# Pairing the two signs of a key feature map in one stationary operand, so that a key-value product moves 65 columns instead of 129

## The chip, the cores and the metric

The kernel runs on one core of one Trainium2 chip. The metric is device time of one execution in microseconds (us), of which several are taken for each kernel, always beside executions of the kernel before on the same chip. The profile also records the mean clock that the throttle granted to TensorE, as a share of full speed (1.000). "PE" is TensorE, "PEld" its weight load, DVE is VectorE, ACT ScalarE, POOL GpSimd, SP SyncE.

## The reference, cut to what matters

Four residual blocks on x of 2048 tokens by 512: attention, feed-forward, attention, feed-forward. The attention is linear, with 32 heads of 16 and two softmaxes of opposite sign as feature map:

```python
pk = jnp.einsum("bhsd,hdf->bhsf", k, w_phi)
phi_k = jnp.concatenate([_softmax(pk, axis=-1), _softmax(-pk, axis=-1)], axis=-1)
kv = jnp.einsum("bhsf,bhsd->bhfd", phi_k, v)        # the key-value products
z  = jnp.einsum("bhsf->bhf", phi_k)
num = jnp.einsum("bhqf,bhfd->bhqd", phi_q, kv)
den = jnp.einsum("bhqf,bhf->bhq", phi_q, z)[..., None] + 1e-6
o = num / den
```

`num` needs the finished `kv`, a sum over all 2048 tokens. Everything after it in the layer waits for the last token tile.

## The kernel before

The kernel is written as a list of operations with the resources that they read and write. A list scheduler in the kernel file orders all of them by given durations, and semaphores are made from that order. So any edit may move every operation.

For each of the 16 token tiles of an attention layer: layer norm, a transpose by DMA, key and value projections (PE), exp with both signs and a copy of v (ACT), the softmax sums and reciprocals (DVE), the multiply that normalises (POOL; for tiles 14 and 15 one half on POOL, one on DVE), then eight key-value products (PE):

```python
    def kv_acc(self, t, tag):
        for g in range(NG):                      # 8 groups: sign s, 8 heads c
            s, c = g // 4, g % 4
            bank, j = g // 3, g % 3              # PSUM banks 0, 1, 2
            op("pe", ... e.matmul(
                k.pb[bank][:, j * 130:j * 130 + 129], k.expk[:, t, s, c * 128:(c + 1) * 128], k.vsb[:, t, c, 0:129],
                start=(t == 0 and j == 0), stop=(t == NT - 1), ...),
               [r("phik", t, s), r("v", t), r("vones")], [self.RP[bank]], 59, f"{tag} kvacc {t} {g}")
```

The stationary operand holds 8 heads of 16 features, the moving one 8 heads of 16 values and a column of ones for `z`. Only the 8 diagonal blocks of the 128x128 result are wanted. The finishing step takes them out of PSUM with a mask, bank by bank:

```python
    def kv_fin(self, tag):
        for bank in range(3):
            ...
            op("dve", ... k.kvbd[:, g0:g0 + n, 0:128] ... pv[:, :, 0:128] ... k.mask8 ..., ALU.mult),
               [self.RP[bank], r("mask8")], [r("kvbd", bank)], 550 if n == 3 else 430, f"{tag} kvbd {bank}")
            op("dve", ... k.kvbd[:, g0:g0 + n, 128:136] ... pv[:, :, 128:129] ..., ALU.add, ALU.mult),
               [self.RP[bank], r("mask8"), r("kvbd", bank)], [r("kvbd", bank)], 200, f"{tag} kvden {bank}")
```

The step runs on DVE once per attention layer. It lets `num` start, and it gives banks 0, 1, 2 back to the query projections, which write to banks 0 to 3.

The softmax here doesn't subtract the row's maximum and nothing guards it: scores larger than these inputs give would overflow.

## Time and profile before

392.31 us in the median of 3 executions (391.47 to 392.65).

From the profile page of the kernel before, engines' busy time and then the chain of work that ended last, by engine:

```profile
PE 379.4 (97%) x2331; PEld 208.0 (53%) x2331; DVE 272.0 (70%) x547; ACT 206.6 (53%) x389; POOL 168.5 (43%) x284
PE 88%; POOL 4%; ACT 3%; DMA 2%; DVE 1%; issue 1%; ACTq 0%; POOLq 0%
```

The timeline at the end of the second attention layer's key phase, kernel before (start, duration, engine and line, what it writes and reads, count, and in brackets the idle time before it with what ended it; L634 is the normalising multiply, L663 the products, L674 and L679 the finishing step, L690 query projections, L706 `num`):

```profile
236.69 1.50 POOL L634 TENSOR_TENSOR expk<-expk,rZk 128x512 bf16<-128x512 bf16 x1 [0.95 <-DVE rZk L631]
237.22 2.77 PE L663 MATMUL ps<-vsb,expk 128*128 128x129 bf16 x45
238.70 1.08 DVE L674 TENSOR_TENSOR kvbd<-ps,mask 128x384 bf16<-128x384 f32 x2 [1.43 <-PE ps L663]
239.70 0.30 DVE L679 SCALAR_TENSOR_TENSOR kvbd<-ps,mask 128x24 bf16<-128x24 f32 x2
239.83 0.38 PE L690 MATMUL ps<-yT,Wqp 128*128 128x512 bf16 x1
240.03 0.42 DVE L674 TENSOR_TENSOR kvbd<-ps,mask 128x256 bf16<-128x256 f32 x1
240.04 0.54 PE L706 MATMUL ps<-kvbd,expq 128*128 128x144 bf16 x6
240.49 0.17 DVE L679 SCALAR_TENSOR_TENSOR kvbd<-ps,mask 128x16 bf16<-128x16 f32 x1
```

How to read it. A matmul's record is long (217 to 231 ns for a product), but records overlap; the cost of one in a row is start to start: 45 products from 237.22 to 239.83 us are 58 ns each. The finishing step begins at 238.70 us, 1.1 us before PE is through with the products and turns to its next matmul (239.83 us), because bank 0 was complete. PE never stops: products, one query projection, then `num`.

### The profile page before, as it was taken

How to read it: one execution, taken by the hardware profiler on the slowest of the kernel's cores; microseconds unless marked ns; L12 is line 12 of the kernel's file. 1: busy time of each engine (PE TensorE's matmuls, PEld its weight loads, DVE VectorE, ACT ScalarE, POOL GpSimd, SP SyncE). 2: the span in 40 equal slices, each digit the busy share in tenths (PEclk: the TensorE clock that was granted, in tenths of full speed). 3: DMA queues.
4: the chain of work that ended last, by engine and by line, in shares of the span. 5: the costliest groups of instructions: out<-in, count | busy, mean ns of one | idle time of the engine just before them, and what ended most of it. 6: DMA issues, size and time to landing. Idle time of an engine off the chain costs nothing.

```text
span 390.3 us, 6397 instructions
## 1 busy us (share of the span) xinstructions
PE 379.4 (97%) x2331; PEld 208.0 (53%) x2331; DVE 272.0 (70%) x547; ACT 206.6 (53%) x389; POOL 168.5 (43%) x284
## 2 busy tenths in 40 slices
PE   5999989999999999999999999999999999999997
PEld 3445554667644544444444457567774554444444
DVE  4999978877766888866766777897986776232222
ACT  5898859834633404533453484985563462553340
POOL 5499936641724363372244543584553242100000
DMA  6833682311311322401000110132323132100002
GB/s 179 228 67 71 191 299 53 69 40 32 53 40 27 43 55 44 84 10 28 14 15 0 27 29 3 40 80 57 55 55 69 27 42 67 29 14 27 17 12 67
DMA packets 61663, 23.01 MB, mean 59 GB/s; under 512 B 53472, under 2 KB 60608, under 8 KB 61632
## 3 DMA queue, kind: packets, MB, share of 16 engines
q1 hardware_dynamic: 60912, 22.02, 24.4%
q10 hardware_dynamic: 720, 0.59, 0.5%
q8 instruction: 18, 0.29, 0.3%
q14 instruction: 13, 0.11, 0.1%
HBM read 7.91 MB, written 2.10 MB: 26 GB/s over the span
## 4 chain that ended last, share of the span: by engine, by line
PE 88%; POOL 4%; ACT 3%; DMA 2%; DVE 1%; issue 1%; ACTq 0%; POOLq 0%
PE ps L758 39%; PE ps L785 19%; PE ps L617 7%; PE ps L737 7%; PE ps L690 6%; PE ps L706 4%; PE ps L663 3%; PE ps L648 2%; POOL expk L634 2%; ACT expq L693 2%; DVE stats L551 1%; DMA x_sb<-in_A_x_dram 1%; DMA hT<-in_A_wqkv_dram 1%; ACT expk L620 1%; POOL rstd L576 1%
## 5 line engine op out<-in xcount | busy, mean ns | idle before, releaser
L758 PE MATMUL ps<-yT,Wg 128*128 128x512 bf16 (+3 forms) x440 | 130.1, 337 | 0.5 <-DMA yT<-ytile 0.2
L758 PE MATMUL ps<-yT,Wu 128*128 128x512 bf16 (+3 forms) x440 | 129.6, 336 | 0.0
L760 ACT ACTIVATE gate_sb<-ps 128x512 bf16<-128x512 f32 (+3 forms) x110 | 55.9, 512 | 105.3 <-PE ps L758 102.9
L785 PE MATMUL ps<-Wd,hT 128*128 128x512 bf16 (+2 forms) x363 | 106.8, 373 | 0.0
L634 POOL TENSOR_TENSOR expk<-expk,rZk 128x1024 bf16<-128x1024 bf16 (+1 forms) x32 | 59.5, 1878 | 37.1 <-DVE rZk L631 19.7
L758 PEld LDWEIGHTS ps<-yT,Wg 128*128 128x128 bf16 (+1 forms) x440 | 43.4, 100 | 33.8 <-issue 1.1
L758 PEld LDWEIGHTS ps<-yT,Wu 128*128 128x128 bf16 (+1 forms) x440 | 43.7, 100 | 32.6 <-ACT expk L765 0.2
L767 DVE TENSOR_TENSOR hT<-gate_sb,expk 128x512 bf16<-128x512 bf16 (+3 forms) x73 | 29.8, 409 | 37.9 <-ACT expk L765 33.0
L785 PEld LDWEIGHTS ps<-Wd,hT 128*128 128x128 bf16 (+1 forms) x363 | 35.3, 98 | 36.6 <-DVE x_sb L787 0.6
L551 DVE BATCH_NORM_STATS2 stats<-x_sb 128x6 f32<-128x512 bf16 x64 | 42.6, 682 | 5.5 <-DMA x_sb<-in_A_x_dram 5.1
L366 ACT ACTIVATE numbf<-ps 128x432 bf16<-128x432 f32 x64 | 33.1, 536 | 19.5 <-PE ps L706 19.4
L629 DVE TENSOR_REDUCE Zk<-expk 128x64 f32<-128x1024 bf16 x32 | 37.7, 1194 | 5.7 <-ACT expk L620 5.4
L731 POOL TENSOR_TENSOR osb<-tsc 128x512 bf16<-128x512 bf16 x28 | 32.5, 1162 | 19.9 <-DVE tsc L726 17.8
L737 PE MATMUL ps<-wo_p,oT 128*128 128x512 bf16 x128 | 39.8, 379 | 0.0
L770 DVE TENSOR_TENSOR hT<-gate_sb,ps 128x512 bf16<-128x512 bf16 (+2 forms) x37 | 22.7, 613 | 20.8 <-PE ps L758 19.6
L693 ACT ACTIVATE expq<-ps 128x1024 bf16<-128x1024 f32 (+1 forms) x40 | 32.6, 861 | 7.3 <-PE ps L690 7.0
L765 ACT ACTIVATE expk<-ps 128x512 bf16<-128x512 f32 (+3 forms) x73 | 36.1, 497 | 0.1
L706 PE MATMUL ps<-kvbd,expq 128*128 128x144 bf16 x256 | 35.0, 226 | 0.5 <-ACT numbf L366 0.5
L620 ACT ACTIVATE expk<-ps 128x512 bf16<-128x512 f32 x44 | 23.9, 598 | 21.5 <-PE ps L617 21.2
L690 PE MATMUL ps<-yT,Wqp 128*128 128x512 bf16 x128 | 34.6, 379 | 0.6 <-ACT expq L693 0.5
L787 DVE TENSOR_TENSOR x_sb<-x_sb,ps 128x512 bf16<-128x512 bf16 (+1 forms) x33 | 22.0, 669 | 18.8 <-PE ps L785 18.4
L559 POOL TENSOR_TENSOR rstd<-rv,mhalf 128x1 f32<-128x1 f32 (+1 forms) x53 | 31.9, 607 | 2.9
(73 smaller groups left out, 429.2 us busy)
## 6 DMA issues: line engine op xcount, KB each, us to landing
out_dram<-x_sb SPq DMA_DIRECT2D x15, 128.0 KB, 1.7
x_sb<-in_A_x_dram SPq DMA_DIRECT2D x3, 512.0 KB, 6.2
Wu<-in_B_W_up_dram SPq DMA_DIRECT2D x4, 344.0 KB, 5.9
Wg<-in_B_W_gate_dram SPq DMA_DIRECT2D x4, 344.0 KB, 5.5
Wd<-in_B_W_down_dram SPq DMA_DIRECT2D x5, 256.0 KB, 6.9
yT<-ytile SPq DMA_TRANSPOSE x60, 2.5
hT<-in_A_wqkv_dram ACTq DMA_DIRECT2D x4, 128.0 KB, 3.1
x_sb<-in_A_x_dram SPq DMA_DIRECT2D x4, 128.0 KB, 3.7
```

Of the source, the lines that this page charges most:

```text
L366: return e.activation(out, in_, ACT.Copy) if hasattr(e, "activation") else e.tensor_copy(out, in_)
L551: op("dve", (lambda t: lambda e: e.bn_stats(k.stats6[:, t, :], k.x_sb[:, t, :]))(t), [r("x", t)], [r("st", t)], 685, f"{tag} stats {t}")
L629: op("dve", lambda e: e.tensor_reduce(k.Zk[:, zb, :], k.expk[:, t, :, :].rearrange("p s (h f) -> p (s h) f", f=16), AX.X, ALU.add), [r("ex ...
L634: op(eng, (lambda s0, s1: lambda e: e.tensor_tensor(k.expk[:, t, s0:s1, :].rearrange("p s (h f) -> p (s h) f", f=16), k.expk[:, t, s0:s1, ...
L690: op("pe", (lambda c, ic, bank: lambda e: e.matmul(k.pb[bank][:], k.Wqp[:, ic, c * 128:(c + 1) * 128], k.yT[:, ic, st * 512:(st + 1) * 512 ...
L693: op("act", (lambda c0, s, b0: lambda e: e.activation(k.expq[:, st, c0:c0 + w, s, :], k.ps[:, b0:b0 + w, :], ACT.Exp, scale=(1.0 - 2.0 * s ...
L706: op("pe", (lambda s, c, j, g0, bank: lambda e: e.matmul(k.pb[bank][:, j * GW:(j + 1) * GW], k.expq[:, st, c, s, tt * 128:(tt + 1) * 128], ...
L737: op("pe", (lambda c, bank: lambda e: e.matmul(k.pb[bank][:], k.oT[:, ob, c, :], k.wo_p[:, c, :], start=(c == 0), stop=(c == NC - 1)))(c, ...
L758: op("pe", (lambda bank, W, ic, fc, Mf: lambda e: e.matmul(k.pb[bank][0:Mf, 0:n], W[:, ic, fc * 128:fc * 128 + Mf], k.yT[:, ic, c0:c0 + n] ...
L760: op("act", (lambda Mf, gb, gs: lambda e: e.activation(k.gate_sb[0:Mf, gs, 0:n], k.pb[gb][0:Mf, 0:n], ACT.Relu))(Mf, gb, gs), [self.RP[gb] ...
L765: op("act", (lambda Mf, ub, tu: lambda e: e.activation(k.expk[0:Mf, tu, 0, 0:n], k.pb[ub][0:Mf, 0:n], ACT.Copy))(Mf, ub, tu), [self.RP[ub] ...
L785: op("pe", (lambda fc, Kf, u, c0, bank, m0, m1: lambda e: e.matmul(k.pb[bank][:, m0:m1], k.hT[0:Kf, u, c0:c0 + 128], k.Wd[0:Kf, fc, m0:m1] ...
```

## The change

Intent: put both signs of four heads (2 x 64 features) into one stationary operand. The moving operand then needs the values of four heads and the ones, 65 columns instead of 129. The number of products stays, their accumulators fit in two banks (0, 1), and bank 2 comes free.

The price is in the finishing step. The rows of a product are now (sign, head of 4), while `num` wants rows of 8 heads per sign, so half of the blocks move by 64 partitions: four multiplies of 64 partitions and four small ones for the denominators, and each reads both banks.

The diff, cut to its core:

```diff
-        sb("expk", [NT, 2, 512])
-        sb("vsb", [NT, NC, 130])
+        sb("expk", [NT, NG, 2, 64])
+        sb("vsb", [NT, NG, 66])
@@ kv_acc
-            s, c = g // 4, g % 4
-            bank, j = g // 3, g % 3
...
-                k.pb[bank][:, j * 130:j * 130 + 129], k.expk[:, t, s, c * 128:(c + 1) * 128], k.vsb[:, t, c, 0:129],
+            bank, col = g // 4, (g % 4 // 2) * 256 + (g % 2) * 66
...
+                k.pb[bank][:, col:col + 65], k.expk[:, t, g, :, :].rearrange("p s m -> p (s m)"), k.vsb[:, t, g, 0:65],
...
-               [r("phik", t, s), r("v", t), r("vones")], [self.RP[bank]], 59, f"{tag} kvacc {t} {g}")
+               [r("phik", t, bank), r("v", t), r("vones")], [self.RP[bank]], KVD, f"{tag} kvacc {t} {g}")    # KVD = 40.0
@@ kv_fin
-        for bank in range(3):
...
-               [self.RP[bank], r("mask8")], [r("kvbd", bank)], 550 if n == 3 else 430, f"{tag} kvbd {bank}")
+        for s in range(2):
+            for u in range(2):
+                src = k.ps[s * 64:s * 64 + 64, 0:2, :] ... u * 66:u * 66 + 65
+                dst = k.kvbd[u * 64:u * 64 + 64, s * 4:s * 4 + 4, :]
...
+                   [self.RP[0], self.RP[1], r("mask4")], [r("kvbd", s, u)], 420, f"{tag} kvbd {s} {u}")
...
+                   [self.RP[0], self.RP[1], r("mask4"), r("kvbd", s, u)], [r("kvbd", s, u)], 200, f"{tag} kvden {s} {u}")
@@ first query projection of the first layer
-        kr0, qr0 = cycle([4, 5, 6, 7]), cycle([3])
+        kr0, qr0 = cycle([4, 5, 6, 7]), cycle([2, 3])
```

Left out: the same new layout in the exps, sums, copies and multiplies, and two setup operations on POOL (a mask, zeros).

More of the change, by code (lines that the diff above doesn't have):

```diff
@@ L360 @@
 EPS_DEN = 1e-6
+KVD = 40.0
 WINDOW = {"sp": 24, "act": 64, "pe": 400, "dve": 40, "pool": 24}
@@ L427, in alloc @@
         sb("mask8t", [8])
+        sb("mask4", [4])
         sb("phi_c", [NC, DH])
@@ L496, in setup @@
         op("pool", lambda e: e.memset(k.aggw[:, 1:2], 1.0 / D), [], [r("aggw")], 100, "agg w1")
-        op("pool", lambda e: e.memset(k.vsb[:, :, :, 128:130], 1.0), [], [r("vones")], 250, "v ones")
+        op("pool", lambda e: e.memset(k.vsb[:, :, :, 64:66], 1.0), [], [r("vones")], 250, "v ones")
+        op("pool", lambda e: e.tensor_tensor(k.mask4[:], k.mask8[:, 0:4], k.mask8[:, 4:8], ALU.add), [r("mask8")], [r("mask4")], 150, "mask4")
+        op("pool", lambda e: e.memset(k.kvbd[:], 0.0), [], [r("kvones")] + [r("kvbd", s, u) for s in range(2) for u in range(2)], 1000, "kvbd zero")
         op("pool", lambda e: e.tensor_copy(k.kvbd[:, :, 136:144], k.mask8[:].unsqueeze(1).to_broadcast([P, NG, 8])), [r("mask8")], [r("kvones")], 230, "kv ones")
@@ L619, in kv_proj @@
         for s in range(2):
-            op("act", (lambda s: lambda e: e.activation(k.expk[:, t, s, :], k.pb[bk][:], ACT.Exp, scale=(1.0 - 2.0 * s)))(s),
+            op("act", (lambda s: lambda e: e.activation(k.expk[:, t, :, s, :], k.pb[bk][:].rearrange("p (g m) -> p g m", g=NG), ACT.Exp, scale=(1.0 - 2.0 * s)))(s),
                [self.RP[bk]], [r("expk", t, s)], 605, f"{tag} expk {t} {s}")
-        op("act", lambda e: e.activation(k.vsb[:, t, :, 0:128], k.pb[bv][:].rearrange("p (c n) -> p c n", c=4), ACT.Copy),
+        op("act", lambda e: e.activation(k.vsb[:, t, :, 0:64], k.pb[bv][:].rearrange("p (g n) -> p g n", g=NG), ACT.Copy),
            [self.RP[bv]], [r("v", t)], 600, f"{tag} vcopy {t}")
@@ L628, in knorm @@
         zb, rb = t % 2, t % 4
-        op("dve", lambda e: e.tensor_reduce(k.Zk[:, zb, :], k.expk[:, t, :, :].rearrange("p s (h f) -> p (s h) f", f=16), AX.X, ALU.add),
+        op("dve", lambda e: e.tensor_reduce(k.Zk[:, zb, :], k.expk[:, t, :, :, :].rearrange("p g s (h f) -> p (g s h) f", f=16), AX.X, ALU.add),
            [r("expk", t, 0), r("expk", t, 1)], [r("Zk", zb)], 1215, f"{tag} Zk {t}")
@@ L632, in knorm @@
         parts = [("pool", 0, 2)] if t < NT - 2 else [("pool", 0, 1), ("dve", 1, 2)]
-        for eng, s0, s1 in parts:
-            op(eng, (lambda s0, s1: lambda e: e.tensor_tensor(
-                k.expk[:, t, s0:s1, :].rearrange("p s (h f) -> p (s h) f", f=16),
-                k.expk[:, t, s0:s1, :].rearrange("p s (h f) -> p (s h) f", f=16),
-                k.rZk[:, rb, s0 * 32:s1 * 32].unsqueeze(2).to_broadcast([P, (s1 - s0) * 32, 16]), ALU.mult))(s0, s1),
-               [r("expk", t, s) for s in range(s0, s1)] + [r("rZk", rb)], [r("phik", t, s) for s in range(s0, s1)],
-               (1930 if s1 - s0 == 2 else 980) if eng == "pool" else 1050, f"{tag} phik {t} {s0}")
+        for eng, u0, u1 in parts:
+            n = (u1 - u0) * 32
+            kv = k.expk[:, t, u0 * 4:u1 * 4, :, :].rearrange("p g s (h f) -> p (g s h) f", f=16)
+            op(eng, (lambda kv, u0, n: lambda e: e.tensor_tensor(
+                kv, kv, k.rZk[:, rb, u0 * 32:u0 * 32 + n].unsqueeze(2).to_broadcast([P, n, 16]), ALU.mult))(kv, u0, n),
+               [r("expk", t, 0), r("expk", t, 1), r("rZk", rb)], [r("phik", t, u) for u in range(u0, u1)],
+               (1930 if n == 64 else 980) if eng == "pool" else 1050, f"{tag} phik {t} {u0}")
     def kv_pair(self, t, ring, tag):
@@ L650, in kv_pair @@
         for s in range(2):
-            op("act", (lambda s: lambda e: e.activation(k.expk[:, t:t + 2, s, :], k.ps[:, kb[0]:kb[0] + 2, :], ACT.Exp, scale=(1.0 - 2.0 * s)))(s),
+            op("act", (lambda s: lambda e: e.activation(k.expk[:, t:t + 2, :, s, :], k.ps[:, kb[0]:kb[0] + 2, :].rearrange("p b (g m) -> p b g m", g=NG), ACT.Exp, scale=(1.0 - 2.0 * s)))(s),
                [self.RP[b] for b in kb], [r("expk", tt, s) for tt in ts], 1030, f"{tag} expk {t} {s}")
-        op("act", lambda e: e.activation(k.vsb[:, t:t + 2, :, 0:128], k.ps[:, vb[0]:vb[0] + 2, :].rearrange("p b (c n) -> p b c n", c=4), ACT.Copy),
+        op("act", lambda e: e.activation(k.vsb[:, t:t + 2, :, 0:64], k.ps[:, vb[0]:vb[0] + 2, :].rearrange("p b (g n) -> p b g n", g=NG), ACT.Copy),
            [self.RP[b] for b in vb], [r("v", tt) for tt in ts], 1030, f"{tag} vcopy {t}")
@@ L660, in kv_acc @@
         for g in range(NG):
-            s, c = g // 4, g % 4
-            bank, j = g // 3, g % 3
-            op("pe", (lambda s, c, bank, j: lambda e: e.matmul(
-                k.pb[bank][:, j * 130:j * 130 + 129], k.expk[:, t, s, c * 128:(c + 1) * 128], k.vsb[:, t, c, 0:129],
-                start=(t == 0 and j == 0), stop=(t == NT - 1), skip_group_check=True))(s, c, bank, j),
-               [r("phik", t, s), r("v", t), r("vones")], [self.RP[bank]], 59, f"{tag} kvacc {t} {g}")
+            bank, col = g // 4, (g % 4 // 2) * 256 + (g % 2) * 66
@@ L668, in kv_fin @@
+            op("pe", (lambda g, bank, col: lambda e: e.matmul(
+                k.pb[bank][:, col:col + 65], k.expk[:, t, g, :, :].rearrange("p s m -> p (s m)"), k.vsb[:, t, g, 0:65],
+                start=(t == 0 and g % 4 == 0), stop=(t == NT - 1), skip_group_check=True))(g, bank, col),
+               [r("phik", t, bank), r("v", t), r("vones")], [self.RP[bank]], KVD, f"{tag} kvacc {t} {g}")
     def kv_fin(self, tag):
         op, r, k = self.op, self.r, self
-        for bank in range(3):
-            g0 = bank * 3
-            n = min(3, NG - g0)
-            pv = k.pb[bank][:, 0:n * 130].rearrange("p (g m) -> p g m", m=130)
-            op("dve", (lambda g0, n, pv: lambda e: e.tensor_tensor(
-                k.kvbd[:, g0:g0 + n, 0:128].rearrange("p g (d h) -> p g d h", h=8),
-                pv[:, :, 0:128].rearrange("p g (h d) -> p g d h", h=8),
-                k.mask8[:].unsqueeze(1).unsqueeze(1).to_broadcast([P, n, 16, 8]), ALU.mult))(g0, n, pv),
-               [self.RP[bank], r("mask8")], [r("kvbd", bank)], 550 if n == 3 else 430, f"{tag} kvbd {bank}")
-            op("dve", (lambda g0, n, pv: lambda e: e.scalar_tensor_tensor(
-                k.kvbd[:, g0:g0 + n, 128:136], pv[:, :, 128:129].to_broadcast([P, n, 8]), 0.5 * EPS_DEN,
-                k.mask8[:].unsqueeze(1).to_broadcast([P, n, 8]), ALU.add, ALU.mult))(g0, n, pv),
-               [self.RP[bank], r("mask8"), r("kvbd", bank)], [r("kvbd", bank)], 200, f"{tag} kvden {bank}")
@@ new lines, in kv_fin @@
+        for s in range(2):
+            for u in range(2):
+                src = k.ps[s * 64:s * 64 + 64, 0:2, :].rearrange("p b (c m) -> p (b c) m", c=2)[:, :, u * 66:u * 66 + 65]
+                dst = k.kvbd[u * 64:u * 64 + 64, s * 4:s * 4 + 4, :]
+                mk = k.mask4[s * 64:s * 64 + 64, :]
+                op("dve", (lambda src, dst, mk, u: lambda e: e.tensor_tensor(
+                    dst[:, :, 0:128].rearrange("p c (d h) -> p c d h", h=8)[:, :, :, u * 4:u * 4 + 4],
+                    src[:, :, 0:64].rearrange("p c (h d) -> p c d h", h=4),
+                    mk.unsqueeze(1).unsqueeze(1).to_broadcast([64, 4, 16, 4]), ALU.mult))(src, dst, mk, u),
+                   [self.RP[0], self.RP[1], r("mask4")], [r("kvbd", s, u)], 420, f"{tag} kvbd {s} {u}")
+                op("dve", (lambda src, dst, mk, u: lambda e: e.scalar_tensor_tensor(
+                    dst[:, :, 128 + u * 4:132 + u * 4], src[:, :, 64:65].to_broadcast([64, 4, 4]), 0.5 * EPS_DEN,
+                    mk.unsqueeze(1).to_broadcast([64, 4, 4]), ALU.add, ALU.mult))(src, dst, mk, u),
+                   [self.RP[0], self.RP[1], r("mask4"), r("kvbd", s, u)], [r("kvbd", s, u)], 200, f"{tag} kvden {s} {u}")
@@ L708, in num @@
                     start=(j == 0), stop=True, skip_group_check=True))(s, c, j, g0, bank),
-                   [r("expq", st, c, s), r("kvbd", gb), r("kvones")], [self.RP[bank]], 63, f"{tag} num {t} {g0 + j}")
+                   [r("expq", st, c, s), r("kvbd", s, 0), r("kvbd", s, 1), r("kvones")], [self.RP[bank]], 63, f"{tag} num {t} {g0 + j}")
             op("dve" if gb == 2 else "act", (lambda g0, n, bank: lambda e: evac(
@@ L763, in step @@
                 tu = 12 + u % 4
-                ru = [r("expk", tu, 0), r("phik", tu, 0)]
-                op("act", (lambda Mf, ub, tu: lambda e: e.activation(k.expk[0:Mf, tu, 0, 0:n], k.pb[ub][0:Mf, 0:n], ACT.Copy))(Mf, ub, tu),
+                ru = [r("expk", tu, 0), r("expk", tu, 1), r("phik", tu, 0)]
+                up = k.expk[:, tu, 0:4, :, :].rearrange("p g s m -> p (g s m)")
+                op("act", (lambda Mf, ub, up: lambda e: e.activation(up[0:Mf, 0:n], k.pb[ub][0:Mf, 0:n], ACT.Copy))(Mf, ub, up),
                    [self.RP[ub]], ru, 170 + n * 0.833, f"{tag} up {ts[0]} {fc}")
-                op("dve", (lambda Mf, tu, gs, u: lambda e: e.tensor_tensor(k.hT[0:Mf, u, 0:n], k.gate_sb[0:Mf, gs, 0:n], k.expk[0:Mf, tu, 0, 0:n], ALU.mult))(Mf, tu, gs, u),
+                op("dve", (lambda Mf, up, gs, u: lambda e: e.tensor_tensor(k.hT[0:Mf, u, 0:n], k.gate_sb[0:Mf, gs, 0:n], up[0:Mf, 0:n], ALU.mult))(Mf, up, gs, u),
                    [r("gate", gs)] + ru, [r("hT", u)], 150 + n * 0.535, f"{tag} h {ts[0]} {fc}")
```

## The prediction

> **What bounds the kernel now.** One core, granted clock 1.000, span 390.3 us. TensorE is listed busy 379.4 us (97%), and the chain that ended last is 88% PE. The key-value products (256 MATMULs of 129 moving columns, half per attention layer) are 2.8% of that chain. In the timeline, 45 of them in a row take 2.61 us (from 237.22): 58 ns each, though each record is 220 ns long. Together: 256 x 58 ns = 14.8 us of TensorE.
>
> The layers differ. In the first (20 to 53 us) POOL is full: its 1.9 us normalisation of expk runs back to back (9 in 16.21 us from 35.78), and the products wait for it; only the last 14, at 52.1 us, stand in the chain. In the second (224.7 to 239.8 us) PE has no gap: 128 products interleaved with projections, ending in the burst of 45. There each nanosecond counts, as long as the chain ACT exp -> DVE sum and reciprocal (1.22 + 0.55 us) -> POOL multiply (1.93 us) for tiles 12 to 15 keeps up.
>
> **Removed.** 64 moving columns per product, not one product: still 256 pairs of weight load and matmul. In proportion 65 columns take 58 x 65/129 = 29 ns, but each product still loads 128 stationary columns. The Trainium skill ("TensorE: Matmul & The Clock Gate", Back-to-back issue gap) says that spacing is set by both instructions, pipelined; this trace shows only that the load's limit is at most 58 ns. My estimate: 40 ns (30 to 54), so 18 ns saved per product: 2.3 us per layer.
>
> **Added.** (a) The finishing step on DVE: before, 3 multiplies (552, 552, 420 ns) and 3 small ones (174 ns), the first starting before the last product was done. After: 4 multiplies of 64 x 256 elements (estimate 420 ns, as the 128x256 one) and 4 small ones, all waiting for both banks. DVE's total is about equal; the first num matmul comes an estimated 0.5 us later, partly covered by query projections. (b) Two POOL setup operations, about 1.2 us; POOL waits for DMA at 2.2 to 3.4 us, so free.
>
> **Moved.** Bank 2 comes free: the first query projection gets two banks, and projections into banks 2 and 3 can run before the finishing step. ACT sits idle 1.5 us before its 54.08 us and 2.4 us before its 240.43 us evacuation, and is 93% busy at 250 to 260 us; an early 1.0 us exp or two fits there. Estimate 0.5 us per layer.
>
> **Sum.** Second layer: -2.3 (products) -0.5 (early exps) +0.4 (finishing) = -2.4 us. First layer: -0.3 -0.5 +0.4 = -0.4 us. The list scheduler reorders everything: +-1.5 us by chance; I add -0.5 us for shorter chains in the second layer. Total about -3.3 us: 389.0 us, 8 in 10 within 386.2 to 391.6. Faster by over 2%: 0.05; within: 0.93; slower by over 2%: 0.02.
>
> **What would show each step.** Burst of products in the timeline: near 40 ns apart (58 = load-bound, 30 = load hidden). From the first product of the second layer to its first num (224.7 to 240.0, 15.3 us) about 2.4 us shorter; the first layer's num start (53.7 us) within 0.7 us. The feed-forward stretches (95 to 215, 270 to 390 us) unchanged in length. Expq on ACT between last product and first numbf.
>
> **What would make it wrong.** Weight loads at 50 ns or more (saving under 1 us). The POOL/DVE chain of tiles 12 to 15 becoming the limit. The finishing step exposed for 1 us or more per layer. A worse order from the scheduler, or a second benefit of the freed bank that I don't see.

## More of the kernel before

How much PE waited for the multiply in the whole run, from the view of waits on PE, kernel before (total us, times, longest):

```profile
PE ps L663 <- POOL expk L634: 0.6, 1, 0.6
```

## The result, and the profile after

The changed kernel gives the right result and takes 395.95 us in the median (394.68 to 396.61, 4 executions), beside 392.27 us for the kernel before: slower by 0.9%. The ratio is 1.0089, with a 95% interval of 1.0067 to 1.011.

The four executions had clocks 0.991 (396.61 us), 0.996 (396.29 and 395.60) and 1.000 (394.68). So there are two losses: about 2.4 us at full clock, and 1 to 2 us more when the clock dropped.

The profile page of the changed kernel: busy time, the granted clock in 40 slices (tenths), the chain by engine:

```profile
PE 376.9 (95%) x2331; PEld 202.0 (51%) x2331; DVE 271.8 (69%) x551; ACT 205.7 (52%) x389; POOL 173.3 (44%) x286
PEclk9999889999999999999999999999999999999999
PE 80%; POOL 6%; DVE 6%; DMA 3%; issue 3%; ACT 1%; SPq 0%; POOLq 0%; DVEq 0%; ACTq 0%
```

PE fell from 88% to 80% of the chain, and DVE rose from 1% to 6%. First, did the products become shorter? The timeline of PE, changed kernel, first layer (L666 the products, L694 a query projection):

```profile
44.81 0.53 PE L666 MATMUL ps<-vsb,expk 128*128 128x65 bf16 x12
45.18 0.38 PE L694 MATMUL ps<-yT,Wqp 128*128 128x512 bf16 x1
```

Twelve products from 44.81 to 45.18 us: 31 ns each. That is better than predicted (40 ns): 27 ns x 256 = 6.9 us of PE are saved. And still the kernel is slower.

The same place of the second layer as shown of before, timeline of the changed kernel (L640 multiply, L626 copy of v, L678 and L683 finishing step, L710 `num`):

```profile
240.16 1.50 POOL L640 TENSOR_TENSOR expk<-expk,rZk 128x512 bf16<-128x512 bf16 x1 [0.95 <-DVE rZk L635]
241.57 0.60 ACT L626 ACTIVATE vsb<-ps 128x512 bf16<-128x512 f32 x1 [1.16 <-PE ps L666]
242.22 0.32 PEld L666 LDWEIGHTS ps<-vsb,expk 128*128 128x128 bf16 x8 [0.29 <-ACT vsb L626]
242.26 0.41 PE L666 MATMUL ps<-vsb,expk 128*128 128x65 bf16 x8
242.74 1.32 DVE L678 TENSOR_TENSOR kvbd<-ps,mask 64x256 bf16<-64x256 f32 x3 [2.00 <-PE ps L666]
244.09 0.36 DVE L683 SCALAR_TENSOR_TENSOR kvbd<-ps,mask 64x16 bf16<-64x16 f32 x2
244.48 0.43 DVE L678 TENSOR_TENSOR kvbd<-ps,mask 64x256 bf16<-64x256 f32 x1
244.51 0.42 PE L710 MATMUL ps<-kvbd,expq 128*128 128x144 bf16 x4 [1.84 <-DVE kvbd L683]
244.94 0.38 DVE L683 SCALAR_TENSOR_TENSOR kvbd<-ps,mask 64x16 bf16<-64x16 f32 x2
```

The finishing step starts only when all products are done. It takes 2.6 us (242.74 to 245.32), and PE stands still for 1.84 us of it before the first `num`. The view of waits on PE has this as its largest entry, and a second new one, a late transpose in the first layer:

```profile
PE ps L710 <- DVE kvbd L683: 3.7, 3, 1.8
PE ps L652 <- DMA yT<-ytile: 2.2, 1, 2.2
```

In this execution the stops were followed by a lower clock. Four windows of the changed kernel (columns: window, its length, busy time of PE, PEld, DVE, ACT, POOL with counts, granted clock, DMA share, GB/s):

```profile
40.00:46.00 6.00, 6.00 (x41) 2.81 (x42) 3.89 (x5) 3.91 (x5) 5.12 (x3) 0.72 0.44 105
56.00:60.00 4.00, 3.19 (x16) 1.81 (x17) 2.09 (x9) 1.90 (x5) 0.00 (x0) 0.65 0.52 162
40.20:43.40 3.20, 3.20 (x9) 1.20 (x8) 1.46 (x2) 1.60 (x2) 3.20 (x3) 0.50 0.39 104
57.30:60.40 3.10, 3.10 (x14) 1.72 (x15) 1.41 (x5) 1.00 (x3) 0.00 (x0) 0.50 0.20 62
```

Each dip follows stops of PE: the wait for the transpose (2.2 us) ended at 39.97 us, the waits for the first layer's finishing step (1.39 and 0.45 us) at 56.35 and 57.23 us. At clock 0.72 and 0.65, 6 us and 4 us hold about 1.7 us and 1.4 us less of PE. The last two lines show that the clock is 0.50 in the dips, each about 3.4 us long. The traces of r4, r5 and r16 below have one such dip each, also at a stop of PE. From this an estimate: a dip is some 1.7 us of lost clock, 0.4% of the run, so a mean clock of 0.996 is one dip, 0.991 two, 0.987 three. But a stop does not always bring a dip: r2's trace has the same wait for the transpose (2.3 us) at clock 1.000.

Where the 4.6 us between the two profiled spans (390.3 and 394.9 us) arise, read from the two timelines:

| moment, us | before | after | difference |
|---|---|---|---|
| first layer: last POOL multiply ends | 51.99 | 53.50 | +1.5 |
| finishing step ends | 54.29 | 57.17 | +2.9 |
| first feed-forward product | 72.12 | 76.39 | +4.3 |
| second layer: last POOL multiply ends | 238.19 | 241.66 | +3.5 |
| finishing step ends | 240.66 | 245.32 | +4.7 |
| first feed-forward product | 257.82 | 263.34 | +5.5 |
| span | 390.3 | 394.9 | +4.6 |

The feed-forward block between the layers gave 0.8 us back, the last one 0.9 us. From the last POOL multiply to the end of the finishing step the two layers took 2.30 and 2.47 us before, 3.67 and 3.66 us after. Not all of that growth is the step's own. In the new order the last products wait for something else: in the second layer for the copy of v, which ends at 242.17 us, 0.51 us after the multiply (shown above), and in the first for the half of a multiply that DVE does, which ends at 54.05 us, 0.55 us after POOL's:

```profile
51.17 2.88 DVE L640 TENSOR_TENSOR expk<-expk,rZk 128x512 bf16<-128x512 bf16 x2
54.10 0.43 PE L666 MATMUL ps<-vsb,expk 128*128 128x65 bf16 x8 [0.56 <-DVE expk L640]
```

Counted from these moments the step ends after 3.12 and 3.15 us, 0.8 and 0.7 us more than before.

### The profile page after: what moved, and what is told of

It reads as the page before. It is cut to its first block, busy times and chain, and to the rows that moved or that the text cites. A ratio compares the mean times of both kernels' runs of the same rounds, so it can differ in the third digit from the quotient of the medians. Undisturbed runs are those within 1.5% of the kernel's fastest.

```text
span 394.9 us, 6391 instructions
## 1 busy us (share of the span) xinstructions
PE 376.9 (95%) x2331; PEld 202.0 (51%) x2331; DVE 271.8 (69%) x551; ACT 205.7 (52%) x389; POOL 173.3 (44%) x286
## 4 chain that ended last, share of the span: by engine, by line
PE 80%; POOL 6%; DVE 6%; DMA 3%; issue 3%; ACT 1%; SPq 0%; POOLq 0%; DVEq 0%; ACTq 0%
PE ps L762 39%; PE ps L790 19%; PE ps L621 7%; PE ps L741 5%; PE ps L694 4%; PE ps L710 3%; DMA yT<-ytile 2%; PE ps L666 1%; DVE stats L555 1%; POOL rstd L563 1%; POOL osb L735 1%; PE ps L652 1%; POOL expk L640 1%; DMA x_sb<-in_A_x_dram 1%; DVE kvbd L678 1%
## 5 line engine op out<-in xcount | busy, mean ns | idle before, releaser
L790 PE MATMUL ps<-Wd,hT 128*128 128x512 bf16 (+2 forms) x363 | 103.1, 373 | 0.0
L640 POOL TENSOR_TENSOR expk<-expk,rZk 128x1024 bf16<-128x1024 bf16 (+1 forms) x32 | 59.1, 1863 | 38.0 <-DVE rZk L635 29.4
L735 POOL TENSOR_TENSOR osb<-tsc 128x512 bf16<-128x512 bf16 x28 | 33.5, 1199 | 15.5 <-DVE tsc L730 14.6
L741 PE MATMUL ps<-wo_p,oT 128*128 128x512 bf16 x128 | 38.8, 379 | 0.8 <-DMA oT<-osb 0.7
L710 PE MATMUL ps<-kvbd,expq 128*128 128x144 bf16 x256 | 33.9, 231 | 5.0 <-DVE kvbd L683 3.7
L694 PE MATMUL ps<-yT,Wqp 128*128 128x512 bf16 x128 | 36.5, 390 | 0.0
L562 POOL TENSOR_SCALAR rv<-mv 128x1 f32<-128x1 f32 (+1 forms) x53 | 13.2, 250 | 50.1 <-DVE mv L557 49.9
```

The lines of the kernel that those rows point to most:

```text
L640: op(eng, (lambda kv, u0, n: lambda e: e.tensor_tensor(kv, kv, k.rZk[:, rb, u0 * 32:u0 * 32 + n].unsqueeze(2).to_broadcast([P, n, 16]), AL ...
L694: op("pe", (lambda c, ic, bank: lambda e: e.matmul(k.pb[bank][:], k.Wqp[:, ic, c * 128:(c + 1) * 128], k.yT[:, ic, st * 512:(st + 1) * 512 ...
L710: op("pe", (lambda s, c, j, g0, bank: lambda e: e.matmul(k.pb[bank][:, j * GW:(j + 1) * GW], k.expq[:, st, c, s, tt * 128:(tt + 1) * 128], ...
L735: op(sm, lambda e: e.tensor_tensor(k.osb[:, b, :], k.tsc[:, b, 0:512], k.tsc[:, b, 512:1024], ALU.add), [r("tsc", b)], [r("osb", b)], 418 ...
L741: op("pe", (lambda c, bank: lambda e: e.matmul(k.pb[bank][:], k.oT[:, ob, c, :], k.wo_p[:, c, :], start=(c == 0), stop=(c == NC - 1)))(c, ...
L790: op("pe", (lambda fc, Kf, u, c0, bank, m0, m1: lambda e: e.matmul(k.pb[bank][:, m0:m1], k.hT[0:Kf, u, c0:c0 + 128], k.Wd[0:Kf, fc, m0:m1] ...
```

## The experiments

Theory A, structural: products of early tiles only fill PE while a chain of other engines runs for the last tiles, so shorter products shorten nothing, while the later and longer finishing step lies on the chain. Theory B, the order: the scheduler made a worse order, which shows in the late transpose and the clock. Theory C: the clock drop comes from PE idling, whatever causes that.

To hold the order fixed, many kernels replace the scheduler by a table of the operations' names:

```diff
-            prog.schedule()
+            prog.fixed(ORDER)      # order from a table; an operation that comes too early for its
+                                   # dependencies is put right after the last of them
```

All kernels, in us. "Full clock" is the mean of the executions at clock 0.999 or more.

| kernel | what | median | ratio (95%) | at full clock |
|---|---|---|---|---|
| after | the change | 395.95 | 1.0089 (1.0067 to 1.011) | 394.68 (1 of 4) |
| r1 | after, old order | 397.89 | 1.0126 (1.0096 to 1.0157) | 394.67 (2 of 6) |
| r2 | after, half the finishing | 393.83 | 1.0053 (1.004 to 1.0067) | 393.67 (4 of 6) |
| r3 | after, 129 columns | 398.28 | 1.0171 (1.0151 to 1.019) | 397.92 (3 of 5) |
| r4 | after, query ring as before | 395.58 | 1.0082 (1.0059 to 1.0104) | 393.85 (2 of 6) |
| r5 | before, 65 columns only | 391.44 | 0.9998 (0.9981 to 1.0016) | 391.48 (5 of 6) |
| r6 | r1 with useless matmuls | 395.85 | 1.0104 (1.0088 to 1.0121) | 395.79 (4 of 4) |
| r7 | after, 4 finishing operations | 395.43 | 1.0101 (1.0075 to 1.0127) | 395.03 (4 of 6) |
| r8 | before, 3 finishing operations | 392.32 | 1.0017 (1.0003 to 1.003) | 392.40 (6 of 6) |
| r9 | after, other banks | 395.30 | 1.0084 (1.0044 to 1.0124) | 394.82 (4 of 5) |
| r10 | before, other banks | 393.33 | 1.0034 (0.9993 to 1.0075) | 392.99 (5 of 6) |
| r11 | after, three mends | 391.84 | 0.9987 (0.9964 to 1.001) | 392.21 (7 of 7) |
| r12 | before, new order | 403.76 | 1.0292 (1.0257 to 1.0328) | 402.34 (2 of 6) |
| r13 | before, late finishing only | 394.50 | 1.0066 (1.005 to 1.0082) | 394.51 (6 of 6) |
| r14 | r1, 4 finishing operations | 394.11 | 1.0053 (1.0038 to 1.0068) | 393.88 (4 of 6) |
| r15 | r1, finishing by bank | 394.28 | 1.0057 (1.004 to 1.0075) | 394.25 (6 of 6) |
| r16 | r9, one look | 395.09 | none (one run) | none (clock 0.996) |
| r17 | after, three mends, four banks | 397.49 | 1.0139 (1.0118 to 1.0159) | 394.95 (1 of 5) |

### r1: the change in the old order

The edit is the table above with the order of the kernel before, the new finishing operations in the places of the old ones. (A few products of one tile trade places, since they share banks otherwise.)

> The changed kernel, but every engine issues its operations in the order that the kernel before had (the order comes from a table; the new finishing operations stand where the old ones stood). Theory A (the finishing step, which now starts only after the last product and must be done before the first num, is exposed: about 1.2 us more per layer than before): even in the old order the gain of the products is eaten, 391.5 to 394 us, and the trace shows PE idle for 1 us or more between last product and first num in both layers. Theory B (the loss is the scheduler's new order, which puts a layer-norm apply late, starves PE at 37 us and drops its clock): 389 us or less, clock 1.000, no 2 us wait for a yT transpose.

Measured: 394.50 and 394.84 us at clock 1.000, and 397.76 to 398.13 us in four executions at 0.986 to 0.991. The wait of 2.2 us for a transpose was gone (0.5 us left), and the kernel was no faster. PE stood idle before the first `num` for 0.75 us in the first layer and 1.20 us in the second (1 us or more was expected in both), and the time lies above the expected range. So the new order (theory B) is not needed for the loss. That the old order suits the new operations is not shown (see r12). At full clock the loss to the kernel before, whose median in those rounds was 391.76 us, is 2.9 us.

### r2: half of the finishing step

```diff
-            for u in range(2):
+            for u in range(1):                     # in kv_fin, after's own order
-        ... e.memset(k.kvbd[:], 0.0)
+        ... e.memset(k.kvbd[:], 1.0)               # keeps the denominators from zero
```

> The changed kernel in its own order, with only half of the finishing step (the u = 1 operations left out; wrong result on purpose). Theory A: first num about 0.9 us earlier after the last product in each layer, and the whole time 1.5 to 2.5 us less than the changed kernel's 395.95 us. Theory B: less than 0.7 us changed.

Measured: wrong result; 393.83 us in the median, 2.1 us under the change, as theory A expected. But at full clock the gain is 1.0 us (393.67 against one execution at 394.68). The rest is clock: four of six executions held full clock, against one of four (whether by the shorter step or by chance is not shown). The step is on the path, for part of its length.

### r3: 129 columns again

```diff
-                k.pb[bank][:, col:col + 65], ..., k.vsb[:, t, g, 0:65],
+                k.pb[bank][:, col:col + 129], ..., k.vsb[:, t, min(g, 6):min(g, 6) + 2, :] ... [:, 0:129],
```

> The changed kernel in its own order, with 129 moving columns per product again (wrong result on purpose; addresses and number of matmuls else the same). Products then take 58 ns instead of 31 ns, 27 ns x 256 = 6.9 us of PE. If PE were the limit while they run: the second layer 3.4 us longer, 399 us or more. If other engines' chains set when the last product can run (theory A's second half): under 1.5 us longer, 396 to 397.5 us.

Measured: 398.28 us; at full clock 3.2 us over the change. Neither expectation was met: 6.9 us more of PE cost about half of it. In this order, planned for 40 ns per product, products of 58 ns seem to hold others up; which, was not traced. That says nothing about the reverse in the kernel before, which r5 tests.

### r4: the query projection in one bank

```diff
-        kr0, qr0 = cycle([4, 5, 6, 7]), cycle([2, 3])
+        kr0, qr0 = cycle([4, 5, 6, 7]), cycle([3])
```

> The changed kernel, rescheduled, with the first query projection in bank 3 alone as before. If the second bank brings query exps between the key exps on ACT and so delays POOL (third theory): 1 us or more faster than 395.95 us. Theory A: within 1 us of it, unless the order happens to move the late layer-norm apply (theory B), which would show as no wait for yT near 37 us and clock 1.000.

Measured: 395.58 us, within 1 us of the change (393.85 us at full clock, in two executions, against one at 394.68). Its new order has no wait for a transpose near 37 us, and the kernel is still slow. The second bank for the first query projection is not the main cause.

### r5: the saving alone

```diff
-                k.pb[bank][:, j * 130:j * 130 + 129], ..., k.vsb[:, t, c, 0:129],
+                k.pb[bank][:, j * 130 + 64:j * 130 + 129], ..., k.vsb[:, t, c, 64:129],   # in the kernel before, its order
```

> The kernel before, in its own order, with its old layout and old finishing step; only the products move 65 columns instead of 129 (columns 64 to 128 of each; wrong result on purpose). This is the saving of the change alone, 256 x 27 ns = 6.9 us of PE, without its cost. Filler theory (the products of tiles 0 to 11 only fill PE while the chain LN - transpose - key projection - exp - sum - multiply of the last tiles runs, so a shorter product shortens nothing): at most 1.2 us faster than 391.76 us, and PE idle of 2 us or more appears before the last products. If PE bound the second layer as the prediction had it: 3 us or more faster, under 388.8 us.

Measured: 391.44 us beside 391.82 us, ratio 0.9998. This is 6.9 us of PE taken out of the kernel before, at no other cost, and nothing clear of the noise came of it (the interval allows -0.7 to +0.6 us). The timeline of PE shows where a part of it went (L806 products, L777 the POOL multiply), second layer, and then its view of waits:

```profile
237.06 0.74 PE L806 MATMUL ps<-vsb,expk 128*128 128x65 bf16 x19
238.93 0.95 PE L806 MATMUL ps<-vsb,expk 128*128 128x65 bf16 x26 [1.14 <-POOL expk L777]
```

```profile
PE ps L806 <- POOL expk L777: 3.2, 4, 1.1
```

The wait for the multiply, 0.6 us in the kernel before, became 3.2 us; the rest of the 6.9 us is not so easily found, since it is spread over shorter waits, some matmul records are missing (2289 of 2331), and this execution had one dip of the clock, at 52 to 55 us. PE had looked gap-free because the scheduler had put the products of earlier tiles into the time in which the last tiles' chain runs. They were filler. Only the products behind the last multiply count: here 26 of them, and 26 x 27 ns = 0.7 us.

### r6: useless matmuls where PE waits

```diff
+    def fill(self, n, tag):      # writes a bank that nobody reads
+        for i in range(n):
+            self.op("pe", lambda e: e.matmul(k.pb[2][:], k.yT[:, 0, 0:128], k.Wkp[:, 0, :], start=True, stop=True), ..., 216, f"{tag} {i}")
+        # r1, q ring [3]; 3 before the products of tiles 12 and 14 of the first layer, 5 after the last product of both
```

> r1 (changed kernel in the old order; five of its runs in two groups: 394.5 and 394.8 us at clock 1.000, 397.8 to 398.1 us at 0.986 to 0.991) with 16 useless 512-column matmuls put on PE where it waits: 3 before the products of tile 12, 3 before those of tile 14, 5 after the last product of each layer (first query projection in bank 3 only, so that bank 2 is free). Clock theory (PE idle around 47 to 55 us makes the clock gate halve the clock): clock 1.000 in all runs and 394 to 395.3 us although PE has 3.5 us more work. If idle is not the cause: two groups as in r1, each the same or up to 3 us slower.

Measured: clock 1.000 in all four executions, 395.35 to 396.11 us. r1 had kept full clock in two of six. The median is 2 us below r1's, with more work on PE, but just above what was expected (394 to 395.3 us). The first layer's critical stretch, r1 at full clock and then r6 (columns as in the windows above):

```profile
46.00:56.70 10.70, 6.90 (x84) 4.04 (x83) 7.34 (x14) 4.31 (x9) 5.27 (x4) 1.00 0.95 333
```

```profile
46.00:56.70 10.70, 9.00 (x93) 5.18 (x93) 7.34 (x14) 4.29 (x9) 5.28 (x4) 1.00 0.93 327
```

PE was busy 6.90 us of 10.70 without the filler and 9.00 us with it. That supports theory C, that PE idling itself takes the clock down, but does not show it: four executions against six are few, r6 also has the other query ring, and both of these traces are at clock 1.00. Against r1 at full clock r6 is 1.1 us slower; which of the fillers cost that was not tested.

### r7 and r8: denominators by the same multiply

```diff
-        sb("vsb", [NT, NG, 66])
+        sb("vsb", [NT, NG, 68])                    # a column of ones per head: 4 x 17 columns
-                k.pb[bank][:, col:col + 65]
+                k.pb[bank][:, col:col + 68]
-                ... four multiplies of 64x256, four of 64x16
+                ... four multiplies of 64x272, denominators among them
```

r8 does the same to the kernel before (136 columns, 3 operations instead of 6). Both are rescheduled.

> The changed kernel, rescheduled, with the denominators made by the same multiply as the numerators (v with a column of ones per head, 68 moving columns, scheduled as 31 ns): 4 finishing operations instead of 8 per layer. Exposed-finishing theory: first num 0.7 to 0.9 us after the last product instead of 1.9 us; 1.5 to 2.5 us faster than the changed kernel (393.5 to 394.5 us), still not faster than before. If the finishing step does not matter: 395 us or more.

> The kernel before, rescheduled, with the denominators made in the same way (136 moving columns): 3 finishing operations instead of 6. Here the step is mostly hidden, so 0 to 1 us faster than 391.76 us; if the finishing step were exposed here too, 1 us or more.

Measured: r7 395.43 us, a miss, with executions from 394.50 to 398.12. Its step is 0.7 us shorter, but the new order had the first layer's last POOL multiply end at 54.54 us in its profile, against 53.50 us in the changed kernel. Two things moved together, so r7 tells nothing; r14 repeats it in a fixed order. r8: 392.32 us beside 391.82, if anything slower (1.0003 to 1.003), where 0 to 1 us faster was expected. No gain of halving the operations shows where the step is mostly hidden; but r8 is rescheduled too, so this is weak.

### r9, r10, r16: a shorter chain for the last tiles

```diff
-                return [...] + [lambda t=t: self.kv_proj(t, mring, "A2") for t in tiles(st)]
+                return [...] + [lambda t=t: self.kv_proj(t, k3ring if st == 3 else mring, "A2") for t in tiles(st)]
+            k3ring = cycle([4, 5])                 # mring = cycle([6, 7]), shared with a query projection
```

r9 is the change with this edit and 31 ns per product in the scheduler; r10 is the kernel before with it; r16 is r9 again, for its trace.

> The changed kernel, rescheduled with 31 ns per product, with one more edit: in the second layer the projections of tiles 12 to 15 write to banks 4 and 5 instead of 6 and 7, which the first query projection uses too at that time. Chain theory (the time to the first num is the chain of the last four tiles' key projection, exp, sum and multiply, and only a shorter chain can turn shorter products into time): last POOL multiply to come 2 us or more earlier after the last feed-forward product than in the changed kernel, 1.5 to 3 us faster than 395.95 us in runs of equal clock. If products or the finishing step alone were the limit: within 0.7 us of the changed kernel.

> The kernel before, rescheduled, with the same edit of banks. There the products, at 58 ns, fill PE in that stretch, so a shorter chain finds no free PE: within 0.8 us of 391.8 us. If the banks alone were the limit, 1.5 us or more faster.

Measured: r9 gained nothing (394.82 us at full clock; one of its executions, the profiled one, 661.88 us at clock 0.561, is not used). r10 was not faster either (393.33 us, interval 0.9993 to 1.0075; within 0.8 us of 391.8 us was expected).

> r9 again, for its trace. If the banks shorten the chain: from the first product of the second layer to the end of the last POOL multiply clearly less than the changed kernel's 15.4 us, 13.5 us or less, and the gain must have been lost after it. If they do not: 15 us or more, and r9's miss is explained.

Measured: the chain did become shorter. The last multiply of the second layer ended 163.7 us after the first layer's first feed-forward product (236.61 less 72.91), against 166.1 us in the kernel before and 165.3 us in the changed kernel. (The measure in the expectation, from the first product on, was a poor one: in this order the first product comes late, and 7.9 us follow.) But the gain was given back at once. From the first `num` to the feed-forward, the kernel before and then r16, as windows:

```profile
240.04:257.82 17.78, 17.51 (x118) 9.24 (x117) 14.87 (x38) 15.83 (x24) 9.03 (x19) 1.00 0.22 46
```

```profile
239.06:259.84 20.78, 17.24 (x114) 8.89 (x114) 16.96 (x41) 17.53 (x27) 9.75 (x21) 0.99 0.22 40
```

The same stretch took 20.78 us instead of 17.78, with no more PE work in it. In it r16's PE waited 1.4 us for transposes of the attention output and 1.0 us for the next layer norm's; the kernel before has no such entry there. In this one trace the time to the end of the layer is set by other waits, on transfers. My step "a shorter chain turns shorter products into time" failed.

### r11 and r17: mends together

r11 has the denominators of r7, the banks of r9, and the finishing step bank by bank (8 operations of 64x136). r17 has four banks for the last projections and the query ring of r4.

```diff
+        for bk in (1, 0):
+            for s in range(2):
+                for u in range(2):
+                    src = k.pb[bk][s * 64:s * 64 + 64, :] ...
+                       [self.RP[bk], r("mask4")], [r("kvbd", s, u, bk)], 290, f"{tag} kvbd {s} {u} {bk}")
```

> The changed kernel with banks 4 and 5 for the last projections, denominators made by the same multiply, and the finishing step done bank by bank (8 operations of 64x136 elements, those of bank 1 able to start while the products of bank 0 run). Chain theory with exposed finishing: faster than the kernel before, 389 to 391.5 us at clock 1.000; PE idle in the first layer can still cost clock (up to 3 us more, told by the clock of each run).

> r11 with four banks (4, 5, 2, 3) for the projections of tiles 12 to 15 in the second layer, and the first query projection in bank 3 alone. If the chain step holds: 389.5 to 391 us at clock 1.000, faster than the kernel before. If it does not: 391.5 to 393 us, as r11.

Measured: r11 391.84 us beside 391.96 us, ratio 0.9987 (0.9964 to 1.001): the same as the kernel before, where faster was expected; some 4 us better than the change in the median and 2.5 us at full clock, which it held in all seven executions. It is the best version of the change that was found, and it does not beat the kernel before. r17 missed: 397.49 us, four of five executions at clock 0.996.

### r12: the kernel before in the new order

The table is r4's order with the old finishing operations in place of the new.

> The kernel before (old products, old finishing step), but in the order of r4, the changed kernel with the query projection in bank 3 as before. It measures the new order by itself. If the order costs nothing: 391.8 us within 0.7. If the order is a large part of the 2.4 to 3.7 us: 393.5 us or more. If it is better, as r4 being no slower than r1 hints: under 391.2 us.

Measured: 403.76 us. By the words of the expectation this would make the order a large part of the loss. I do not read it so, because 12 us is far more than there is to explain: the order was made for shorter products and other banks, and in it PE waits 3.8 us for query exps and 3.2 us for the finishing step (`L833` in its view of waits), where the kernel before waits 0.5 us and not at all. It says that an order need not carry over. r1 goes in the kinder direction, since there the products became shorter, but its finishing step is longer and needs both banks, so r1 may be hurt a little by its order as well.

### r13: the late finishing step alone

```diff
-               [self.RP[bank], r("mask8")], [r("kvbd", bank)], 550 ...
+               [self.RP[0], self.RP[1], self.RP[2], r("mask8")], [r("kvbd", bank)], 550 ...     # and the small ones; in the kernel before, its order
```

> The kernel before, own order, old products and layout; only its six finishing operations now wait for the last product of all three banks (as the changed kernel's do for both of its banks). Finishing theory: the end of the step moves from about 0.6 us to 1.7 us or more after the last product, in both layers, 393.3 to 395 us. If the late finish is not the cause: 391.8 us within 0.6.

Measured: 394.50 us beside 392.00 us, ratio 1.0066 (1.005 to 1.0082), full clock in all six executions. The old six operations, the old products, the old order; the only change is that each operation of the step waits for all three banks, and so also holds all three until the step has read them. That alone costs 2.5 us. Its timeline in the second layer (L817 and L822 the step, L849 `num`) to be compared with that of before:

```profile
237.84 2.59 PE L806 MATMUL ps<-vsb,expk 128*128 128x129 bf16 x42
240.46 1.02 DVE L817 TENSOR_TENSOR kvbd<-ps,mask 128x384 bf16<-128x384 f32 x2 [2.75 <-PE ps L806]
241.63 0.55 PE L849 MATMUL ps<-kvbd,expq 128*128 128x144 bf16 x6 [0.99 <-DVE kvbd L822]
```

In the kernel before the step began 1.1 us before PE was through with the products, and now it begins after them. PE stops for 1 us. Query projections could fill it, but by the edit those into banks 0 to 2 are held until the step has read all three. How the 2.5 us divide between the later first `num` and the later banks was not tested.

### r14 and r15: a shorter step in a fixed order

r14 is r7's edit in r1's order, r15 the bank-by-bank step of r11 in r1's order (bank 0 first).

> r1 (changed kernel, old order) with the denominators made by the same multiply: 4 finishing operations instead of 8, nothing else moved. Finishing theory: step ends 0.7 to 0.9 us earlier after the last product in each layer; in runs at clock 1.000 392.8 to 393.8 us against r1's 394.5 and 394.8. Otherwise within 0.4 us of r1.

> r14 with the step done bank by bank (8 operations of 64x136 elements; those of bank 0 can start before the last products of bank 1), order else as r1. Finishing theory: first num 0.3 us or more earlier than in r14, but bank 0 is given back to the query projection only after 6 operations; at clock 1.000 392 to 393.5 us, no slower than r14 by more than 0.3 us. It should not beat the kernel before by more than 0.5 us, since the products only fill.

The step on DVE in the first layer, timelines of r1 and then r14:

```profile
52.23 0.86 DVE L821 TENSOR_TENSOR kvbd<-ps,mask 64x256 bf16<-64x256 f32 x2 [1.87 <-PE ps L809]
53.12 0.36 DVE L826 SCALAR_TENSOR_TENSOR kvbd<-ps,mask 64x16 bf16<-64x16 f32 x2
53.52 0.88 DVE L821 TENSOR_TENSOR kvbd<-ps,mask 64x256 bf16<-64x256 f32 x2
54.43 0.39 DVE L826 SCALAR_TENSOR_TENSOR kvbd<-ps,mask 64x16 bf16<-64x16 f32 x2
```

```profile
53.09 1.85 DVE L821 TENSOR_TENSOR kvbd<-ps,mask 64x272 bf16<-64x272 f32 x4 [1.87 <-PE ps L809]
```

Measured: the step went from 2.59 us (52.23 to 54.82) to 1.85 us, and the time at full clock from 394.67 to 393.88 us: 0.8 us for 0.74 us in each of two layers, about half, and just short of the 392.8 to 393.8 us that were expected. r15 is no faster than r14 (394.25 at full clock, 0.75 us above what was expected). Its step starts earlier but is longer (2.59 us in the first layer, 52.56 to 55.15). Counted from the last multiply, its first `num` came earlier (after 1.36 and 1.32 us in the two layers, not 1.91 and 2.31), and nothing came of that. So the moment of the first `num` is not all that counts. The end of the step, which gives the last bank back, came no earlier (after 3.07 and 3.32 us, not 2.80 and 3.21).

### What adds up

At full clock the change costs 2.4 us (one execution, 394.68 less 392.27) to 2.9 us (r1, two executions, 394.67 less 391.76). By single experiments in the old order: the late start of the finishing step with its held banks +2.5 us (r13), its greater length +0.8 us (r1 less r14), the shorter products -0.3 us (r5 at full clock, 391.48 less 391.82; its interval holds zero). The sum is +3.0 us, so with executions scattering by some 0.5 us nothing of size is missing for r1. For the changed kernel in its own order the parts are less certain: there r3 puts the same 27 ns per product at 3.2 us, r2 puts half of the step at 1.0 us, and the trace shows a multiply and a copy of v, each some 0.5 us late in the new order. That it comes out like r1 may be partly chance. On top comes the clock, +1.1 us in the mean of the change's four executions (395.8 less 394.7) and up to 3.5 us in r1. That idling takes the clock down is supported by the dips, which all follow stops of PE, and by r6, but is not shown: r15 held full clock in six of six executions without any filler. Why the same kernel drops in some executions and not in others stays open.

## Why the prediction was wrong

- **"Removed": the product.** Predicted 40 ns (30 to 54), measured 31 ns: right in the range, too cautious in the middle. The weight load does not show. This made the predicted saving larger, not smaller.
- **"There each nanosecond counts": the step that failed.** It was read from a PE without gaps in the second layer. -2.3 us were expected of the second layer. r5 took 27 ns from each of 256 products in both layers and gained 0.3 us at full clock, within the noise; instead PE waited longer for the multiply (3.2 us, not 0.6). The prediction's own test failed too: from the first product of the second layer to its first `num` took 18.3 us (226.22 to 244.51), not 2.4 us less than 15.3 us. The condition was named ("as long as the chain ... keeps up"), but I treated it as met. The Trainium skill ("Perfetto Trace Analysis", Identifying the Most-Contended Engine) says that matmul busy time is no good measure of how close PE is to roofline, because its instructions are pipelined. The figure misleads, for a further reason: at 97% busy, 6.9 us less PE work changed nothing, because that work was filler. The test that the profile offered was the chain of the last tile, which ends at 238.19 us with 1.85 us to the first `num`.
- **"Added" (a): mis-sized, and the cover was missing.** "0.5 us later, partly covered": from the last input of the last products to the first `num` it was 1.69 and 1.85 us before and 2.30 and 2.34 us after, so 0.6 and 0.5 us later, about as predicted. But nothing covered it: PE stood still for 1.39 and 1.84 us before the first `num`. And the step cost more than that delay: +2.5 us for its late start and held banks (r13) and +0.8 us for its length (r1 less r14), 3.3 us in all, where the sum had 0.8 us (0.4 per layer). Its exposure for 1 us or more was named among the dangers. The step took 2.6 us, since a multiply of 64x256 costs 0.43 us like one of 128x256, and all four depend on the last product. That DVE's total is "about equal" was true and beside the point: what counted was when the step could begin.
- **"Moved": half right.** An early query exp did run before the first evacuation, on ACT at 242.46 us. No gain of it shows: from the first `num` to the feed-forward took 18.8 us (244.51 to 263.34) instead of 17.8 us.
- **"The list scheduler reorders everything: +-1.5 us by chance".** r1 goes back to the old order and stays slow at full clock. r7 against r14 shows such chance at work (395.03 and 393.88 us at full clock, same operations, other order).
- **Not foreseen at all: the clock.** The Trainium skill ("TensorE: Matmul & The Clock Gate", Part 1) describes a gate that halves the clock after an idle window of 3.4 us. The halving is in the traces here: the dips of the changed kernel are at clock 0.50. The idle before them was shorter than the page's window: 2.2 us before the first, 1.39 and 0.45 us before the second. Here a change that shortened PE work in a stretch limited by other engines made PE idle, and in the executions with a dip that was charged a second time.

## What to carry to other kernels

A busy engine without gaps may be full of filler: before making its work shorter, ask which chain ends the stretch, and test it by shrinking the work alone, even with a wrong result, before building the change around it. A step at a join (all tiles done, next phase may start) counts by when its last input arrives and what it holds back, not by its total. Giving up an early start on one bank cost 2.5 us here (r13); but winning it back with twice as many operations gained nothing (r15), so look at when the step ends, too. And where PE becomes idle, look at the granted clock of each execution, since the loss may be twofold.

## What the Trainium skill lacked or had wrong

- "TensorE: Matmul & The Clock Gate", Back-to-back issue gap: it gives about 81 ns per matmul for a stream of load and matmul pairs at N=128 and says that N/2.4 + 2.5 undercounts there. Here such pairs took 58 ns at 129 columns and 31 ns at 65 columns (12 in 0.37 us), within 2 ns of that formula (56.3 and 29.6 ns). The load of 128 columns was hidden even at 65.
- The same page, "Why this matters for your kernels": it advises no PE-idle gap of more than about 3 us. Here a stop of 2.2 us was followed by half clock (0.50 from 40.2 to 43.4 us, the changed kernel), while the same stop of 2.3 us in r2's trace was not. The longest single wait of PE in the key phase of r1's trace (taken at full clock) is 1.2 us, with PE busy 6.90 of 10.70 us, and four of six executions of that kernel fell to a mean clock of 0.986 to 0.991; with 9.00 of 10.70 us busy (r6) none of four did, with 8.01 us (r15) none of six. The page does not say what busy share within a window keeps the clock.
- The same page: it tells of a clock stuck for some 50 us. One execution of r9 ran at about half clock from the second fortieth of its profile to the end (mean 0.561, 661.88 us), with PE busy 97% of the span. No page tells of that.
- "Perfetto Trace Analysis", Optimizing Scalar/DVE Operations: it says that breaking up instructions may let work complete sooner where DVE causes bubbles on other engines. r15 did so to the finishing step and gained nothing over r14 (394.25 against 393.88 us at full clock): its eight operations took 324 ns each, r14's four of twice the size 463 ns each, so the step began earlier but, counted from the last multiply, ended 0.1 to 0.3 us later.
